# Attention loads of 256 tokens of one batch, and attention products on 64x64 tiles of TensorE

## The chip, the cores and the metric

The kernel runs on one core of a Trainium2 chip. The metric is the device time of one execution in microseconds, the median of several runs. The core has five engines that run their own instruction streams in order: TensorE (PE, the matmuls; its weight loads are listed apart as PEld), VectorE (DVE), ScalarE (ACT), GpSimd (POOL) and SyncE (SP, which here only issues DMAs). Matmuls write to PSUM, which has eight banks; the other data lie in SBUF, 128 partitions wide.

## The reference

A linear attention with decay (the RetNet recurrence) makes x, and a two-layer perceptron with a tanh gelu follows. There are 4 batches, 8 heads, 768 tokens and 64 elements a head, so 3072 rows of 512; the hidden width is 2048.

```python
for t in range(S):
    state = gamma * state + k[t] (outer) v[t]        # per batch and head, 64 x 64
    y[t] = scale * q[t] @ state
x = y as (batch * token, head * 64)
h = x @ w_in                                          # 512 -> 2048
g = 0.5 * h * (1 + tanh(c * (h + 0.044715 * h**3)))
out = g @ w_out                                       # 2048 -> 512
```

All inputs and the output are float32.

## The kernel before, in words

**Units of work.** The 768 tokens are cut into six chunks of 128. One chunk of all four batches (512 tokens) is one unit `c`. For each unit and batch, attention is done in chunked form: scores A = k q^T for all heads (`mm_A`, line 252), masked and scaled on VectorE into `a_sb` (`ev_A`, 265); the output Y is the sum of the carry product from the state `st` (`mm_yc`, 276) and the inner product of `a_sb` and v (`mm_yi`, 289), copied out to `xT` (`ev_Y`, 305 or 180/182); the new state is k^T v (`mm_s`, 313) added to the decayed old one (`ev_S`, 330). `att_AY` (348) issues the carry products of one pair of batches, the scores of another and the inner products in one go.

**Tiles on TensorE.** A head has 64 elements. The scores use two row halves of the array (64x128), inner products and states two column halves (128x64), the carry product the two diagonal 64x64 quarters. Each score matmul covers 128 keys and 128 queries of one head.

**Transposes.** Scores need q and k with the head's elements on the partitions. In units 0 and 1 TensorE transposes them (`mm_T`, 229). For q from unit 2 and for k from unit 3 on the load itself brings 32x32 blocks into place (`load_blk`, 106, 16 DMAs of 64 KB with runs of 128 bytes) and VectorE transposes within the blocks (238); k is then loaded a second time in its natural layout (`load1`, 100, runs of 256 bytes) for the states.

**The perceptron.** `moe1` (and `moe1_two`, on half the tokens) computes 128 columns of h in PSUM banks "h" (398) and ScalarE writes its gelu to `g` (414). Unit 0 multiplies by w_out directly (`moe2`, 432). From unit 1 on, `units_w` uses a Strassen-Winograd scheme: seven products of half size, each in two steps a = 0, 1 (536), over sums of g (`g_sums`, 476, on GpSimd, on VectorE in the last unit) and sums of w_out (`w_sums`, 469, VectorE). Step n = 2 is the first product that reads the sums.

**Order.** The order on each engine is written by hand. `run` (597) issues a list of TensorE units, and after unit i the entries of a table. The table of unit 1 (732 to 769) and the loop over units 2 to 5 (772 to 803) place the attention of the next unit and the preparation of the one after between matmuls of the perceptron. Scalings and casts of q, k and v (`prep1`, `prep_blk`) run on ACT, POOL and DVE. POOL's list at the end of unit 1 is: the sums, v of two batches, the last four sums, v of the other two, then v of unit 3.

**DMA queues.** Loads go through SP in order (some early ones through ACT), weights through POOL. At unit 0's end SP stores three output blocks (`ev_O`, 448 to 456) and goes on to load unit 2 at line 733. A one-element copy (`hold`, 130) makes the load of unit 1 wait until the third part of w_out has landed.

Of the kernel before, what the change touches and what calls it, by code (L numbers as in the profile page):

```python
# [16 lines left out]
def kernel(  # L17
# [12 lines left out]
    NCk = S // C  # L30
# [4 lines left out]
    assert Dh == 64 and d_model == H * Dh and B == 4 and NHP == 4 and NF == 16  # L35

    gam = 1.0 - 2.0 ** (-5.0 - np.arange(H, dtype=np.float64))
    p_i = np.arange(128, dtype=np.float64)  # L40
    qdec = gam[None, :] ** (p_i[:, None] - 32.0) * 0.125
    kdec = gam[None, :] ** (160.0 - p_i[:, None])
    g128 = gam ** 128.0
    gst = np.where(p_i[:, None] < 64, g128[None, 0::2], g128[None, 1::2])
    tri = (p_i[:, None] <= p_i[None, :]).astype(np.float64)

    j_p = np.arange(128)[:, None] // 64
    cst_np = np.concatenate([qdec, kdec, gst, tri], axis=1).astype(np.float32)
# [3 lines left out]
    hp_a, t_a = np.arange(NHP)[None, :, None], np.arange(128)[None, None, :]  # L52
    dec_np = 0.125 * gam[2 * hp_a + j_p[:, :, None]] ** (t_a - 32.0)
# [4 lines left out]
    ld = ctx.enter_context(tc.tile_pool(name="ld", bufs=2 * B))  # L58
    pre = ctx.enter_context(tc.tile_pool(name="pre", bufs=2 * B))
    att = ctx.enter_context(tc.tile_pool(name="att", bufs=4))  # L60
    xp = ctx.enter_context(tc.tile_pool(name="xp", bufs=1))
# [4 lines left out]
    OQ, OK, OG, OT = 0, H, 2 * H, 2 * H + NHP  # L66


    misc = const.tile([128, 32], F32)
    cst = const.tile([128, 192], F32)  # L70
    iden = const.tile([128, 128], F16)
    dec = const.tile([128, NHP, 128], F32)

    raw = {}
    srcs = {"q": q, "k": k, "v": v}

    BLK = {"q": (2, 3, 4, 5), "k": (3, 4, 5)}

    def ld_all(key):
        if key not in raw:
            raw[key] = ld.tile(
                [128, B * NHP, 4, 32],
                F32,
                tag=key[0],
                bufs=2 if key[0] == "q32" else 1,
                name=key[0],
            )
        return raw[key]  # L90

    def ld_tile(nm, c, b):
        if nm == "q":
            t = ld_all(("q32", c)).rearrange("p (b hp) a d -> p b (hp a d)", b=B)
            return t[:, b].rearrange("p (h d) -> p h d", h=H)
        if (nm, c, b) not in raw:
            raw[nm, c, b] = ld.tile([128, H, Dh], F32, tag=f"{nm}32", bufs=8, name=f"{nm}32")
        return raw[nm, c, b]

    def load1(eng, nm, c, b):  # L100
        eng.dma_start(  # L101
            out=ld_tile(nm, c, b),
            in_=srcs[nm][b, :, c * C:(c + 1) * C, :].rearrange("h p d -> p h d"),
        )

    def load_blk(nm, c):
        t = ld_all((nm + ("32" if nm == "q" else "T32"), c))
        src = srcs[nm].rearrange("b (hp j) s (dd d) -> j dd s (b hp) d", j=2, dd=2)
        for j in range(2):
            for dd in range(2):  # L110
                for a in range(4):
                    p0, t0 = (2 * j + dd) * 32, c * C + a * 32
                    nc.sync.dma_start(  # L113
                        out=t[p0:p0 + 32, :, a, :], in_=src[j, dd, t0:t0 + 32]
                    )

    def load(c):
        load_blk("q", c)
        if c in BLK["k"]:
            for b in range(B):  # L120
                load1(nc.sync, "v", c, b)
            load_blk("k", c)
            for b in range(B):
                load1(nc.sync, "k", c, b)
        else:
            for b in range(B):
                for nm in "kv":
                    load1(nc.sync, nm, c, b)

    def hold(nm, c, b, until):  # L130

        nc.gpsimd.tensor_copy(out=ld_tile(nm, c, b)[0:1, 0, 0:1], in_=until)

    nc.sync.dma_start(out=cst[:, :OT + 128], in_=cst_h.ap())
    load1(nc.scalar, "q", 0, 0)
    load1(nc.sync, "k", 0, 0)
    load1(nc.scalar, "v", 0, 0)
    nc.sync.dma_start(out=iden, in_=iden_h.ap())
    load1(nc.sync, "q", 0, 1)
    load1(nc.scalar, "k", 0, 1)  # L140
    load1(nc.sync, "v", 0, 1)
    load1(nc.sync, "k", 0, 2)
    load1(nc.sync, "q", 0, 3)
    load1(nc.sync, "v", 0, 3)


    zero = const.tile([128, 512], F16, name="zero")
    nc.vector.memset(zero, 0.0)  # L148
    nc.scalar.activation(
        out=misc[:, 0:1], in_=zero[:, 0:1], func=AF.Gelu_apprx_tanh, scale=1.0  # L150
    )

    def spin(n):
        ps = bank("h", shape=(128, 512), name="spin_ps")
        for _ in range(n):
            nc.tensor.matmul(  # L156
                out=ps, lhsT=zero[:, 0:128], rhs=zero, start=True, stop=True
            )


    st = const.tile([128, B, NHP, 64], F16, name="st")


    mask = const.tile([128, 2, NHP, 128], F32, name="mask")
    for j in range(2):
        for hp in range(NHP):
            nc.vector.tensor_scalar(
                out=mask[:, j, hp],
                in0=cst[:, OT:OT + 128],
                scalar1=float(1.0 / g128[2 * hp + j]),  # L170
                scalar2=None,
                op0=ALU.mult,
            )

    h16 = {}
    blk16 = {}

    def copy_on(eng, out, in_):
        if eng is nc.scalar:
            eng.copy(out=out, in_=in_)  # L180
        else:
            eng.tensor_copy(out=out, in_=in_)

    def prep1(eng, nm, c, b):
        t = pre.tile(
            [128, H, Dh], F16, tag=f"{nm}16", bufs=6 if nm == "q" else 2 * B, name=f"{nm}16"
        )
        src = ld_tile(nm, c, b)
        if (nm == "v") == (c < 2):
            copy_on(eng, t, src)  # L190
        else:
            col = OQ if nm == "q" else OK
            eng.tensor_tensor(  # L193
                out=t,
                in0=src,
                in1=cst[:, col:col + H].unsqueeze(2).broadcast_to([128, H, Dh]),
                op=ALU.mult,
            )
        h16[nm, c, b] = t

    def prep_blk(eng, nm, c, b):
        key, tag = ("q32", "q16") if nm == "q" else ("kT32", "kT16")
        t = pre.tile([128, NHP * 4, 32], F16, tag=tag, bufs=6 if nm == "q" else B, name=tag)
        copy_on(
            eng, t, ld_all((key, c))[:, b * NHP:(b + 1) * NHP].rearrange("p hp a d -> p (hp a) d")
        )
        blk16[nm, c, b] = t

    def pair(t, hp):
        return t[:, 2 * hp:2 * hp + 2]  # L210
# [6 lines left out]
    BANKS = {"h": 2, "o": 2, "att": 4}  # L217

    def bank(tag, dt=F32, shape=(128, NHP, 128), name="ps"):
        return psum.tile(list(shape), dt, tag=tag, bufs=BANKS[tag], name=name)  # L220

    def mm_T(c, b):
        parts = [(i, nm) for i, nm in enumerate("qk") if c not in BLK[nm]]
        if not parts:
            return
        ps = bank("att", F16, (128, 2, NHP, 128), "qkT_ps")
        for i, nm in parts:
            for hp in range(NHP):
                nc.tensor.transpose(  # L229
                    out=ps[:, i, hp], in_=pair(h16[nm, c, b], hp), identity=iden  # L230
                )
        pss["T", c, b] = ps

    def ev_T(c, b, eng=nc.vector):
        t = att.tile([128, 2, NHP, 128], F16, tag="qkT", name="qkT")
        for i, nm in enumerate("qk"):
            if c in BLK[nm]:
                nc.vector.transpose(  # L238
                    out=t[:, i].rearrange("p hp t -> p (hp t)"),
                    in_=blk16.pop((nm, c, b)).rearrange("p ha d -> p (ha d)"),  # L240
                )
        if ("T", c, b) in pss:
            i0 = sum(c in BLK[nm] for nm in "qk")
            copy_on(eng, t[:, i0:], pss.pop(("T", c, b))[:, i0:])
        qkT[c, b] = t

    def mm_A(c, b):
        t = qkT[c, b]
        ps = [bank("att", name=f"a_ps{j}") for j in range(2)]
        for hp in range(NHP):  # L250
            for j in range(2):
                nc.tensor.matmul(  # L252
                    out=ps[j][:, hp],
                    lhsT=t[j * 64:(j + 1) * 64, 1, hp],
                    rhs=t[j * 64:(j + 1) * 64, 0, hp],
                    start=True,
                    stop=True,
                )
        pss["A", c, b] = ps

    def ev_A(c, b):
        ps = pss.pop(("A", c, b))
        for j in range(2):
            s = att.tile([128, NHP, 128], F16, tag=f"a{j}", name=f"a_sb{j}")
            nc.vector.tensor_tensor(out=s, in0=ps[j], in1=mask[:, j], op=ALU.mult)  # L265
            a_sb[c, b, j] = s
# [567 lines left out]
```

## Time and profile before

| | us |
|---|---|
| median of 3 runs | 211.73 (211.6 to 213.02) |
| span of the profiled execution | 209.7 |
| TensorE busy | 200.6 |
| first projection matmul (unit 0) | 16.72 |
| output product of unit 0 begins | 32.92 |
| first projection of unit 1 | 51.94 |
| loops of units 2, 3, 4 and 5 begin | 88.15, 119.08, 149.66, 179.53 |
| last matmul ends | about 205.7 |
| one 128x512 sum on GpSimd / scaling of v | 1.15 / 1.04 |
| stream transposes on VectorE (28) | 19.1 in all |

The span is the time from the first to the last instruction of one profiled execution; the measured time is a little longer. In the timelines the first column is the start and the second the length of a merged piece; pieces of matmuls overlap a little, as their ends are modelled, so starts are compared with starts. "idle before" names how long the engine stood still and what released it.

| group | count | busy us | mean ns |
|---|---|---|---|
| projection (398) | 488 | 87.4 | 334 |
| scores (252), 64x128 tiles | 192 | 8.1 | 218 |
| carry (276), 64x64 tiles | 160 | 6.7 | 220 |
| inner (289), 128x64 tiles | 192 | 8.6 | 223 |
| states (313), 128x64 tiles | 160 | 5.1 | 198 |
| transposes (229) | 80 | 7.8 | 219 |

The mean of one matmul holds its way through the array; several are under way at once.

### The profile page before, as it was taken

The page shows a single profiled execution, that of the slowest core. Times are in us where ns is not written, and L with a number is a line of the kernel's source. Part 1 is how long each engine was busy: PE and PEld are TensorE (multiplying, and loading weights), DVE is VectorE, ACT ScalarE, POOL GpSimd, SP SyncE. Part 2 cuts the span into 40 slices and gives each one's busy share as a digit, 9 for nine tenths or more (in the row PEclk, how much of TensorE's full clock was granted, in tenths as well). Part 3 has the DMA queues.
Part 4 walks back from the last instruction along what each step waited for, and adds up shares of the span by engine and source line. Part 5 has one row for each costly group of instructions (what it writes and reads, how often), then busy time and mean ns, then how long its engine had stood idle before and what let it go on. Part 6 is the DMA issues. An engine that isn't in the chain of part 4 may idle for free.

```text
span 209.7 us, 4776 instructions
## 1 busy us (share of the span) xinstructions
PE 200.6 (96%) x1928; PEld 132.0 (63%) x1928; DVE 104.1 (50%) x213; ACT 101.9 (49%) x182; POOL 115.4 (55%) x120
## 2 busy tenths in 40 slices
PE   7789999999998999999999999999999999999992
PEld 3347644456786878844688744678644788545881
DVE  4445153478734649703857630867432784053430
ACT  2474563144458615168745266643365811566311
POOL 0596001133099999249998299997499980200000
PEclk9999999999999999999999999999999999999999
DMA  7999999998899798799798698796970000500004
GB/s 168 287 253 207 206 205 222 273 269 215 157 220 233 110 179 163 110 313 177 124 219 128 124 340 131 125 207 99 206 251 0 0 3 0 203 0 0 0 28 177
DMA packets 124438, 33.19 MB, mean 158 GB/s; under 512 B 117952, under 2 KB 122432, under 8 KB 124416
## 3 DMA queue, kind: packets, MB, share of 16 engines
q1 hardware_dynamic: 108272, 21.09, 50.3%
q0 software_dynamic: 5456, 8.65, 17.4%
q10 hardware_dynamic: 10688, 3.15, 6.4%
q8 instruction: 15, 0.25, 0.4%
q14 instruction: 7, 0.06, 0.1%
HBM read 30.78 MB, written 6.29 MB: 177 GB/s over the span
## 4 chain that ended last, share of the span: by engine, by line
PE 81%; SPq 6%; ACT 4%; DMA 4%; DVE 2%; issue 1%; ACTq 1%; DVEq 0%
PE h_ps L398 35%; PE o_ps L536 29%; SPq L113 5%; PE o_ps L432 5%; PE a_ps L252 3%; PE y_ps L289 3%; PE y_ps L276 2%; DMA iden<-rr_ident 2%; DMA v<-in_v_dram 2%; PE qkT_ps L229 2%; PE spin_ps L156 1%; SPq L101 1%; PE s_ps L313 1%; ACT g L414 1%; ACTq L101 1%
## 5 line engine op out<-in xcount | busy, mean ns | idle before, releaser
L398 PE MATMUL h_ps<-xT,w_in 128*128 128x512 f16 (+2 forms) x488 | 87.4, 334 | 0.5 <-ACT g L414 0.5
L414 ACT ACTIVATE g<-h_ps 128x512 f16<-128x512 f32 (+1 forms) x98 | 57.5, 589 | 33.9 <-PE h_ps L398 33.5
L398 PEld LDWEIGHTS <-w_in 128*128 128x128 f16 x488 | 45.3, 97 | 37.4 <-issue 2.8
L467 POOL TENSOR_TENSOR s_g<-g 128x512 f16<-128x512 f16 x32 | 36.9, 1152 | 9.4 <-ACT g L414 9.4
L265 DVE TENSOR_TENSOR a_sb<-a_ps,mask 128x512 f16<-128x512 f32 x48 | 30.1, 682 | 23.1 <-PE a_ps L252 23.1
L536 PEld LDWEIGHTS <-s_g 128*128 128x128 f16 x320 | 30.2, 98 | 4.3
L536 PE MATMUL o_ps<-t_w,s_g 128*128 128x256 f16 x240 | 27.8, 273 | 0.0
L536 PEld LDWEIGHTS <-g 128*128 128x128 f16 x240 | 23.4, 98 | 3.6
L467 POOL TENSOR_TENSOR s_g<-s_g,g 128x512 f16<-128x512 f16 x16 | 18.4, 1153 | 1.3
L536 PE MATMUL o_ps<-w_out,g 128*128 128x256 f16 x160 | 18.6, 273 | 0.0
L467 POOL TENSOR_TENSOR s_g<-g,s_g 128x512 f16<-128x512 f16 x16 | 18.5, 1153 | 0.0
L193 POOL TENSOR_TENSOR k<-k,cst 128x512 f16<-128x512 f32 x8 | 8.3, 1044 | 17.3 <-DMA k<-in_k_dram 17.3
L569 POOL DMA_DIRECT2D out_dram<-o_sb x8 | 5.9, 737 | 20.3 <-DVE o_sb L467 16.8
L193 POOL TENSOR_TENSOR v<-v,cst 128x512 f16<-128x512 f32 x16 | 16.2, 1044 | 0.0
L238 DVE STREAM_TRANSPOSE qkT<-kT 128x512 f16<-128x512 f16 x12 | 8.1, 678 | 15.0 <-ACT kT L180 9.5
L565 ACT COPY o_sb<-o_ps 128x512 f32<-128x512 f32 (+1 forms) x5 | 2.7, 543 | 25.1 <-PE o_ps L536 25.1
L432 PE MATMUL o_ps<-w_out,g 128*128 128x512 f16 x64 | 14.8, 380 | 0.0
L305 DVE TENSOR_TENSOR xT<-y_ps,dec 128x512 f16<-128x512 f32 x16 | 10.3, 686 | 4.5 <-PE y_ps L289 4.5
L238 DVE STREAM_TRANSPOSE qkT<-q 128x512 f16<-128x512 f16 x16 | 11.0, 690 | 2.6 <-ACT q L180 2.5
L559 ACT COPY s_u<-o_ps 128x512 f32<-128x512 f32 (+1 forms) x6 | 3.1, 514 | 17.6 <-issue 9.9
L330 DVE SCALAR_TENSOR_TENSOR st<-st,cst,s_ps 128x128 f16<-128x128 f16 (+1 forms) x40 | 10.1, 313 | 2.0 <-PE s_ps L313 2.0
L156 PE MATMUL spin_ps<-zero 128*128 128x512 f16 x32 | 9.4, 429 | 1.2 <-DVE zero L148 1.2
(55 smaller groups left out, 185.3 us busy)
## 6 DMA issues: line engine op xcount, KB each, us to landing
k<-in_k_dram SPq DMA_DIRECT2D x22, 256.0 KB, 4.7
v<-in_v_dram SPq DMA_DIRECT2D x18, 256.0 KB, 4.0
q<-in_q_dram SPq DMA_DIRECT2D x64, 64.0 KB, 2.8
out_dram<-o_sb POOLq DMA_DIRECT2D x8, 512.0 KB, 5.2
kT<-in_k_dram SPq DMA_DIRECT2D x48, 64.0 KB, 2.7
w_in<-in_moe_w_in_dram POOLq DMA_DIRECT2D x4, 512.0 KB, 9.3
w_out<-in_moe_w_out_dram POOLq DMA_DIRECT2D x4, 512.0 KB, 14.7
v<-in_v_dram ACTq DMA_DIRECT2D x6, 256.0 KB, 5.5
```

The lines of the kernel that those rows point to most:

```text
L113: nc.sync.dma_start(out=t[p0:p0 + 32, :, a, :], in_=src[j, dd, t0:t0 + 32])
L156: nc.tensor.matmul(out=ps, lhsT=zero[:, 0:128], rhs=zero, start=True, stop=True)
L193: eng.tensor_tensor(out=t, in0=src, in1=cst[:, col:col + H].unsqueeze(2).broadcast_to([128, H, Dh]), op=ALU.mult,)
L238: nc.vector.transpose(out=t[:, i].rearrange("p hp t -> p (hp t)"), in_=blk16.pop((nm, c, b)).rearrange("p ha d -> p (ha d)"),)
L265: nc.vector.tensor_tensor(out=s, in0=ps[j], in1=mask[:, j], op=ALU.mult)
L305: nc.vector.tensor_tensor(out=x, in0=ps, in1=dec, op=ALU.mult)
L330: nc.vector.scalar_tensor_tensor(out=t[:, :, hp], in0=t[:, :, hp], scalar=cst[:, OG + hp:OG + hp + 1], in1=s_ps[:, :, hp], op0=ALU.mult, o ...
L398: nc.tensor.matmul(out=out, lhsT=w_in_sb[wi][:, kc, wr * 128:(wr + 1) * 128], rhs=xT[c][:, kc, t0:t1], start=(kc == 0), stop=(kc == NHP - ...
L414: nc.scalar.activation(out=out, in_=in_, func=AF.Gelu_apprx_tanh, scale=1.0)
L432: nc.tensor.matmul(out=ps[:, n0:n1], lhsT=g_sb[c, fc // 8][:, fc % 8, b * C:(b + 1) * C], rhs=w_out_sb[fc // (NF // NO)][:, fc % (NF // NO ...
L467: eng.tensor_tensor(out=out, in0=in0, in1=in1, op=op)
L536: nc.tensor.matmul(out=po, lhsT=lhs(c, lk, fp, a), rhs=rhs(rk, fp), start=(new and fp == 0 and (last or a == 0)), stop=(stop and fp == NP ...
```

## The change

**Units and loads.** A unit `m` is now 256 tokens of two batches (`pb`): units 0 and 1 cover the first 256 tokens, 2 and 3 the next, 4 and 5 the last. A load brings 256 tokens of one batch: partition p holds the neighbouring tokens 2p and 2p + 1 (r = 0, 1), so a run is 512 bytes and a load 512 KB. Partitions 0 to 63 are the first chunk of 128 tokens (cc = 0), 64 to 127 the second. `load_blk` and the second load of k are gone, and so are the VectorE transposes.

**Transposes.** In units 0 and 1 TensorE transposes q and k as before. From unit 2 on q and k are cast and SP issues a transposing DMA from SBUF to SBUF for each (16 of 256 KB).

```diff
+    def T_dma(nm, m, bi):
+        SY.dma_start_transpose(out=qk_tile(m, bi)[:, "qk".index(nm)], in_=h_tile(nm, m, bi))
```

**Products.** A chunk's keys (and queries) of one parity r and half cc are 64 long. Scores, inner products and states are matmuls with 64 rows and 64 columns, in the order x, r, j, cc, so that four in a row lie on four quarters of the array. There are twice as many as before; the carry product keeps its count.

```diff
+    QUADS = [(x, r, j, cc) for x in range(2) for r in range(2) for j in range(2) for cc in range(2)]
+
+    def A_mm(m, bi, us=(0, 1)):
+        t = qk_tile(m, bi)
+        for u in us:
+            ps = [bank("att", shape=(128, 2, 2, 128), name=f"a_ps{j}") for j in range(2)]
+            pss["A", m, bi, u] = ps
+            for x, r, j, cc in QUADS:
+                n = 2 * (2 * u + x)
                 nc.tensor.matmul(
-                    out=ps[j][:, hp],
-                    lhsT=t[j * 64:(j + 1) * 64, 1, hp],
-                    rhs=t[j * 64:(j + 1) * 64, 0, hp],
+                    out=ps[j][half(cc), x, r],
+                    lhsT=t[half(j), 1, n + r, half(cc)],
+                    rhs=t[half(j), 0, n:n + 2, half(cc)],
                     start=True,
                     stop=True,
                 )
```

Because carry and inner products write the same bank from different row halves, a one-element copy on ACT or DVE now reads the bank after the last carry product, and the first inner product waits for it:

```diff
+        dst, src = misc[0:1, 1:2], ys[1][0:1, NHP - 1, 0:1]
+        seen = eng.copy(out=dst, in_=src) if eng is AC else eng.tensor_copy(out=dst, in_=src)
+        needs(seen, ins)
+        behind[m, bi] = seen
```

`slot` takes the place of `att_AY`: carry of (m, bi), scores of another half, inner products, copies out, masks. The state step of both chunks is `S_mm` and `S_ev` (tensor_tensor operations where scalar_tensor_tensor stood); `v` is decay-scaled in place of k, the mask is one triangle for all heads, and `xT` has two buffers.

**Order.** The tables are rewritten. Unit 0's output product runs in the order of halves n = 0, 1, then 2, 3 (before: 0, 1, 2 side by side, then 3). Loads of (2, 0), (2, 1) and (3, 0) stand on SP behind unit 0's stores and ahead of the first transposes. Those of unit 1:

```diff
+    loads(2, 0)
+    loads(2, 1)
+    loads(3, 0)
     run(
...
         {
+            2: [(slot, 1, 1, "o", VE, None, None, (VE, AC))],
+            3: [(g_sums, PO, 1, 0, 4, 0, 1), (casts, VE, 2, 0), (T_dmas, 2, 0)],
+            6: [(casts, VE, 2, 1), (T_dmas, 2, 1), (loads, 3, 1)],
             7: [(g_sums, PO, 1, 4, 8, 0, 1)],
+            10: [(att_A, 2, 0)],
+            11: [(g_sums, PO, 1, 0, 4, 1, 2)],
+            12: [(scale_v, PO, 2, 0)],
+            15: [(g_sums, PO, 1, 4, 8, 1, 2), (scale_v, PO, 2, 1)],
         },
     )
     run(
         units_w(1),
         {
+            0: [(casts, AC, 3, 0), (T_dmas, 3, 0), (loads, 4, 0)],
+            2: [(casts, AC, 3, 1), (T_dmas, 3, 1), (loads, 4, 1)],
+            4: [(att_S, 2)],
+            6: [(slot, 2, 0, "h", AC, 2, 1), (scale_v, PO, 3, 0)],
+            9: [(slot, 2, 1, "h", AC, 3, 0), (scale_v, PO, 3, 1)],
+            13: [(att_S, 3)],
         },
     )
```

and those of the loop over units 2 to 5:

```diff
         for i in range(4):
+            more(4 * i + 3, (g_sums, PO if n < NM else VE, c, 2 * i, 2 * i + 2))
+        if n < NM:
+            more(6, (slot, n, 0, "o", VE, n, 1))
+            more(22, (slot, n, 1, "h", AC, m, 0))
+        if m < NM:
+            more(15, (casts, AC, m, 0), (T_dmas, m, 0))
+            more(23, (casts, AC, m, 1), (T_dmas, m, 1))
+            more(15, (scale_v, PO, m, 0), (scale_v, PO, m, 1))
+            more(28, (att_S, m))
+        if m + 1 < NM:
+            more(15, (loads, m + 1, 0))
+            more(23, (loads, m + 1, 1))
```

## The prediction

> **What bounds the kernel now.** I read the page's busy shares first, then the chain of waits, then TensorE's timeline, and last the timelines of the engines that feed it.
>
> ```profile
> PE 200.6 (96%) x1928; PEld 132.0 (63%) x1928; DVE 104.1 (50%) x213; ACT 101.9 (49%) x182; POOL 115.4 (55%) x120
> ...
> PE 81%; SPq 6%; ACT 4%; DMA 4%; DVE 2%; issue 1%; ACTq 1%; DVEq 0%
> ```
>
> TensorE is busy 96% of 209.7 us, so time is won only by shortening its stream and lost by any new wait in it. TensorE's timeline, start and length in us:
>
> ```profile
> 51.94 1.92 PE L398 MATMUL h_ps<-xT,w_in 128*128 128x256 f16 x16
> ...
> 76.47 0.63 PE L276 MATMUL y_ps<-qkT,st 64*64 64x128 f16 x16
> 77.03 0.62 PE L252 MATMUL a_ps<-qkT 64*128 64x128 f16 x16
> 77.58 0.64 PE L289 MATMUL y_ps<-a_sb,v 128*64 128x128 f16 x16
> 78.15 2.79 PE L536 MATMUL o_ps<-t_w,s_g 128*128 128x256 f16 x24
> 80.88 0.44 PE L313 MATMUL s_ps<-v,k 128*64 128x64 f16 x16
> 81.25 1.92 PE L536 MATMUL o_ps<-t_w,s_g 128*128 128x256 f16 x16
> ...
> 87.99 4.39 PE L398 MATMUL h_ps<-xT,w_in 128*128 128x512 f16 x19
> ```
>
> Read start to start. 16 attention matmuls take 0.55 us. Elsewhere 8 of the same take 0.33 us (chain of waits), so 8 more cost 0.22: two tiles run together, 55 ns a pair, plus about 0.11 us whenever the tile shape changes. The state products (64 columns) take 0.25 for 8 and 0.37 for 16: 31 ns a pair. A projection unit of 8 matmuls of 256 columns takes 0.875 us.
>
> Two feeders run with no slack beside this: GpSimd and the load queue.
>
> ```profile
> 57.45 1.14 POOL L467 TENSOR_TENSOR s_g<-g 128x512 f16<-128x512 f16 x1 [5.71 <-ACT g L414]
> ...
> 71.56 2.05 POOL L193 TENSOR_TENSOR v<-v,cst 128x512 f16<-128x512 f32 x2
> ...
> 77.02 1.15 POOL L467 TENSOR_TENSOR s_g<-g,s_g 128x512 f16<-128x512 f16 x1
> 78.13 6.05 POOL L193 TENSOR_TENSOR v<-v,cst 128x512 f16<-128x512 f32 x6
> ```
>
> From 57.45 GpSimd is packed: 16 sums at 1.13 us, with two v scalings before the last four sums. Its sums end at 78.13, and TensorE reads them at 78.15. The state products at 80.88 read the v scaled at 71.56. SyncE's queue:
>
> ```profile
> 44.10 1.77 SPq L455 DMA_DIRECT2D out_dram<-o_sb  x3
> 45.92 0.82 SPq L732 DMA_DIRECT2D dec<-rr_dec  x1
> 46.83 10.59 SPq L113 DMA_DIRECT2D q<-in_q_dram  x16
> 57.47 0.49 SPq L101 DMA_DIRECT2D k<-in_k_dram  x1
> ```
>
> Loads for chunk 2 start behind the third store, at 46.83, 22.5 us before TensorE's first score product of that chunk (69.33).
>
> **Work on TensorE.** Scores, inner outputs and states go from pairs to twice as many matmuls on four tiles; the carry product stays in pairs. If four run as one, the four-tile group streams in 55 ns what the pair did; if only pairs overlap it takes 110. The tightest spacing in the trace is 15 to 16 ns a matmul (states), four of which make 62 ns: I take 60. The TensorE work of the second stage (start of unit 1's first projection, 51.94, to the loop, 88.15: 36.2 us) becomes: 30 projection units at about 0.87 = 26.2; the second half's outputs of unit 1, 0.9; scores of (2,0), 0.6; two slots of carry 0.44 + scores 0.48 + inner 0.48 + switches 0.15 = 3.1; two state products of 64 matmuls, 16 x 31 to 62 ns, 0.9 each with switches. Sum 32.6, so 3.6 less than now. The saving is k's transposes (0.23 each, with waits of 0.45, 0.32 and 0.48 before them) and tile-shape switches that vanish because carry, scores and inner outputs now share one shape.
>
> A rule speaks against the change here. The Trainium skill (TensorE: Matmul & The Clock Gate, Part 3) lets a weight load overlap a running matmul only where the row group differs, and two of the four tiles share a row group. In this trace the inner outputs and states share all rows, differ in column half only, and still run as pairs at 55 and 31 ns: measurement and rule differ, the measurement decides for two tiles, and nothing here shows four.
>
> **New wait 1: transposes behind loads.** From unit 2 on, q and k are transposed by DMA on SyncE's queue. For (2,0) they stand behind nine loads of 512 KB, which stand behind the third store of unit 0. That store now follows the 15th of 16 output steps, so the loads start only 1.7 us before unit 1's first projection (call its start T): after that step come the copy 0.6 and store issue 0.6 on one side, and slot 1.45 + last step 0.86 + states 0.6 on TensorE. Scores of (2,0) are wanted after 11 projection steps and the slot: T + 10.5. The queue is first in, first out by the chain's own row for the 32 KB identity matrix, which took 4.28 us behind larger loads. Rate: loads of 256-byte runs reach 287 GB/s (5 to 10 us). Queue 10 (nearly all 256-byte) spends 20 ns a packet; taking these out of queue 1 leaves about 12.4 for 128 bytes; the line gives 33.7 ns at 512, so 1.16 times the rate: 330 GB/s. Nine loads take 14.3 us. No row shows a DMA transpose: bounds are the plain rate (0.8 us each) and the slow 128-byte loads (16 x 64 KB in 10.59 us, so 2.65 us each). I take the plain one. Landing: T - 1.7 + 2 (start and landing) + 14.3 + 1.6 = T + 16.2: TensorE waits 5.7 us. For the transpose's price the Trainium skill has two answers: "TRN2 transpose DMAs are as fast as regular DMAs" (Advanced Engine Details and Errata, X-Bar Transpose), which gives the sum above, and 1309 ns per 128x128 block (VectorE: DVE Perf Modes, The three transpose paths), which for eight blocks in turn would be an estimated 10.5 us each, 168 us for the sixteen, and a kernel far above 250 us; no run here shows either.
>
> **New wait 2: states behind GpSimd.** The states of unit 2 now stand after the fifth output step of unit 1 and read v of (2,1), whose scaling is GpSimd's last piece after all 16 sums. Were TensorE never to wait, it would come there at T + 20.4 (16 projection steps 14.0, slot 0.9, scores 0.6, five output steps 4.35, the first batch's states 0.55). GpSimd starts at T + 5.3 (four steps 3.5, slot 0.9, gelu and hand-over 0.9), does 16 x 1.13 + 2 x 2.05 = 22.2 plus 0.4 of waiting as now: T + 27.9, 7.5 us late even without wait 1. With wait 1 the third group of sums starts after its gelu at T + 16.2 + 0.6 + 0.875 + 0.65 = T + 18.3, and GpSimd ends 13.2 us later (9.1 of sums, 4.1 of v): T + 31.5. Both waits together cost 31.5 - 20.4 = 11.1.
>
> After idling TensorE is slow: the spin matmuls at the start come every 0.43 us for 2.5 us, then every 0.22. Two such restarts: the first delays GpSimd about 0.7, the second costs 1.3.
>
> **The three loops.** The third output product reads GpSimd's sums pair by pair. TensorE reaches its seventh pair at 18.9 + 0.65 us from a loop's start (16 projections 13.8, one slot 1.55, four output steps 3.5, six matmuls 0.65), but GpSimd, with an unchanged start of 4.3 and 14 sums, is ready at 20.4 (now 108.53 - 88.15). What scores and slots save ahead of that point is lost to it; behind it stands as much as now. Loops: 30.7, 30.6, 29.5 against 30.93, 30.58, 29.87, so -0.5.
>
> **Start.** First projection now at 16.72. Bytes ahead of the first 256 tokens are the same 1.5 MB and the k cast of (0,1) stands on ScalarE ahead of the first outputs' copies; longer runs save about a microsecond of loading, bigger pieces lose it again. The weights still pace the reload of unit 1 (GpSimd's wait for w_out, 14.44 us). VectorE must wait for bigger q tiles before the transposes of (1,1). T = 52.5, between 50 and 55: +0.6.
>
> The added one-element reads between carry and inner products are hidden under scores or a projection step in nine slots and bare in three, about 0.2 us each (the 128x1 ACTIVATE takes 0.20): +0.6. They queue on ScalarE and VectorE in order, behind a cast at most. Removed and hidden: VectorE's stream transposes (28, 19 us), the second load of k, the smaller packets; none is on the path now.
>
> Sum: 0.6 - 3.6 + 11.1 + 2.0 - 0.5 + 0.6 = +10.2. Span 209.7 becomes 219.9; the median stands 2.0 above the span: 221.9, rounded to 221.5.
>
> **Rivals.**
> 1. Transposes in time, GpSimd alone late: loads above 450 GB/s or overtaken in the queue. 7.5 + 1.3 in place of 13.1: 217. Against: the identity row. 0.12.
> 2. Slow transposes (2.65 us): wait 1 grows by 3.7, and in two loops scores of the next unit wait 1.6 each: 228. 0.12, of which 0.02 for transposes slower still, by which the loops themselves would wait. The skill's 1309 ns belongs to that last case.
> 3. Four tiles go as two pairs, 110 ns: 192 groups of scores and inner outputs + 50 ns = 9.6, states little; a third is hidden before GpSimd's two points: 228 to 231. The skill's row-group rule above would do this or worse. 0.10.
> 4. Faster: neither wait comes, TensorE keeps its 3.6 and the loops' 0.5. This decides if GpSimd ends by T + 20.4, i.e. sums and scalings at two thirds of their present time, or TensorE comes 7 us later for a cause that does not prolong the rest, and the transposes land by T + 10.5: 211.7 + 0.6 - 3.6 - 0.5 + 0.6, about 209. For it: lighter DMA and VectorE. Against: GpSimd's rows are its own speed, not waiting. 0.10.
> 5. Part of this, within 1% of 211.7: 0.06.
>
> The forecast keeps 0.50. Slower by over 1% (about what a measurement can tell from no change): 0.50 + 0.12 + 0.12 + 0.10 = 0.84; faster 0.10; same 0.06. Range 214 to 231: it holds cases 1 to 3 and the start's spread, and leaves out 4 and 5.
>
> **What would show it.** TensorE idle before the first four-tile scores of unit 2 until a DMA, about 6 us; idle in the states of unit 2 until GpSimd, about 5 us; four-tile score groups of 32 in about 0.5 us; in the loops short waits for GpSimd's sums. A stage from T to the loop of 45 us is right, 33 wrong. If TensorE comes to the states after GpSimd, or transposes land within 4 us of their cast, the forecast falls.

## The result, and the profile after

The changed kernel takes 236.88 us (median of 4 runs, 235.65 to 237.8) against 212.38 us of the kernel before beside it (4 runs, 211.6 to 213.15): a ratio of 1.116, 95% interval 1.110 to 1.122. It is slower, as forecast, but by 24.5 us and not by 10; the time lies above the range of 214 to 231. Experiment 11 alone had slower executions (three of ten, at 217 us and more); its time below is the median of the other seven.

The profiled execution spans 233.9 us (before: 209.7). The page's busy times and its chain of waits:

```profile
PE 203.4 (87%) x2440; PEld 134.2 (57%) x2440; DVE 93.4 (40%) x173; ACT 95.1 (41%) x158; POOL 110.0 (47%) x101
...
PE 51%; POOL 22%; DMA 17%; DVE 3%; SPq 2%; ACT 2%; issue 1%; POOLq 0%; DVEq 0%
```

TensorE does about as much work as before (203.4 us against 200.6) but holds only 51% of the chain, where it held 81%; GpSimd and DMA take 39% of it. Where the time went, by starts of TensorE's pieces in the two timelines:

| from, to | before us | after us | difference |
|---|---|---|---|
| start to unit 0's output product | 32.92 | 34.57 | +1.65 |
| to unit 1's first projection (T) | 19.02 | 25.10 | +6.08 |
| T to the loop of unit 2 | 36.05 | 50.65 | +14.60 |
| loops of units 2, 3, 4 | 30.92, 30.59, 29.86 | 31.44, 31.46, 30.63 | +2.16 |
| the last unit, to the end of the span | 30.34 | 30.05 | -0.29 |

The loop starts given at the top for the kernel before, and taken over by the prediction (36.2 us for T to the loop), are those of the chain of waits, 0.16 to 0.17 us later than in the timeline; the table reads both kernels in the timeline.

TensorE's timeline of the changed kernel (start, length, engine and line, operation, and in brackets the idle time before it and what ended it):

```profile
59.67 2.83 PE L401 MATMUL h_ps<-xT,w_in 128*128 128x256 f16 x24
...
79.24 1.07 PE L227 MATMUL a_ps<-qkT 64*64 64x128 f16 x32 [7.59 <-DMA qkT<-q]
80.24 5.39 PE L401 MATMUL h_ps<-xT,w_in 128*128 128x256 f16 x40
...
95.77 0.64 PE L270 MATMUL s_ps<-v,k 64*64 64x64 f16 x32 [5.40 <-POOL v L137]
96.35 3.24 PE L540 MATMUL o_ps<-t_w,s_g 128*128 128x256 f16 x16
...
110.32 6.26 PE L401 MATMUL h_ps<-xT,w_in 128*128 128x512 f16 x28
...
131.28 2.14 PE L540 MATMUL o_ps<-t_w,s_g 128*128 128x256 f16 x18 [1.18 <-POOL s_g L137]
```

T is 59.67. The two forecast waits stand in the second stage, at 79.24 for the DMA that transposes q, and at 95.77 for GpSimd's v. After each, TensorE runs slow: the 32 scores at 79.24 take 1.00 us up to the next piece (0.57 in experiment 1 below), and the 16 matmuls of 256 columns at 96.35 take 3.17 instead of 1.75. The mean granted clock of this stage, as a share of TensorE's full speed, is 0.87, where it was 1.00 before. In each of the three loops a wait of 1.16 to 1.18 us for GpSimd's sums is new.

SyncE's queue (the first two columns are start and length of the issue, stalls included):

```profile
46.34 10.49 SPq L463 DMA_DIRECT2D out_dram<-o_sb  x3
56.88 0.43 SPq L93 DMA_DIRECT2D k<-in_k_dram  x1
...
70.05 1.51 SPq L93 DMA_DIRECT2D v<-in_v_dram  x1
71.66 4.10 SPq L216 DMA_TRANSPOSE qkT<-k  x1
75.86 1.36 SPq L216 DMA_TRANSPOSE qkT<-q  x1
```

The loads start at 56.88 behind the third store, 2.8 us before T. The ninth is issued at 70.05, and only then the two transposes, as the program orders them.

GpSimd's timeline:

```profile
75.12 1.15 POOL L137 TENSOR_TENSOR s_g<-g,s_g 128x512 f16<-128x512 f16 x1
82.84 1.15 POOL L137 TENSOR_TENSOR s_g<-g 128x512 f16<-128x512 f16 x1 [6.58 <-ACT g L417]
...
92.71 1.15 POOL L137 TENSOR_TENSOR s_g<-g,s_g 128x512 f16<-128x512 f16 x1
93.82 6.07 POOL L137 TENSOR_TENSOR v<-v,cst 128x1024 f16<-128x1024 f32 x3
```

GpSimd itself stands still for 6.58 us, because TensorE, waiting for the transposes, produces no h from which ScalarE could make g. It then works without a gap to the v that TensorE waits for at 95.77. So GpSimd can't use the first wait to catch up, and the second comes nearly whole on top of it: 5.40 us here, 5.96 in experiment 1, where most of the first is gone.

### The profile page after: what moved, and what is told of

Same layout as the page of the kernel before. It is cut to its first block, busy times and chain, and to the rows that moved or that the text cites. A ratio compares the mean times of both kernels' runs of the same rounds, so it can differ in the third digit from the quotient of the medians.

```text
span 233.9 us, 5567 instructions
## 1 busy us (share of the span) xinstructions
PE 203.4 (87%) x2440; PEld 134.2 (57%) x2440; DVE 93.4 (40%) x173; ACT 95.1 (41%) x158; POOL 110.0 (47%) x101
## 3 DMA queue, kind: packets, MB, share of 16 engines
q0 software_dynamic: 5456, 8.65, 16.2%
## 4 chain that ended last, share of the span: by engine, by line
PE 51%; POOL 22%; DMA 17%; DVE 3%; SPq 2%; ACT 2%; issue 1%; POOLq 0%; DVEq 0%
PE h_ps L401 20%; PE o_ps L540 20%; POOL s_g L137 18%; DMA w_out<-in_moe_w_out_dram 6%; DMA v<-in_v_dram 5%; PE a_ps L227 3%; POOL v L137 2%; DMA k<-in_k_dram 2%; PE o_ps L435 2%; PE y_ps L332 2%; PE y_ps L313 2%; SPq L216 2%; DMA q<-in_q_dram 2%; DVE a_sb L137 2%; PE s_ps L270 1%
## 5 line engine op out<-in xcount | busy, mean ns | idle before, releaser
L401 PE MATMUL h_ps<-xT,w_in 128*128 128x512 f16 (+1 forms) x480 | 87.2, 339 | 2.5 <-DMA w_in<-in_moe_w_in_dram 0.9
L417 ACT ACTIVATE g<-h_ps 128x512 f16<-128x512 f32 x96 | 57.4, 598 | 46.7 <-PE h_ps L401 46.7
L137 DVE TENSOR_TENSOR a_sb<-a_ps,cst 128x512 f16<-128x512 f32 x48 | 29.8, 680 | 12.8 <-PE a_ps L227 12.7
L540 PE MATMUL o_ps<-t_w,s_g 128*128 128x256 f16 x240 | 29.7, 281 | 3.5 <-POOL s_g L137 3.5
L137 POOL TENSOR_TENSOR v<-v,cst 128x1024 f16<-128x1024 f32 (+1 forms) x14 | 23.4, 1685 | 18.3 <-DMA v<-in_v_dram 18.3
L540 PE MATMUL o_ps<-w_out,g 128*128 128x256 f16 x160 | 18.3, 273 | 0.0
L132 ACT CAST k<-k 128x1024 f16<-128x1024 f32 (+1 forms) x11 | 10.1, 928 | 17.1 <-DMA k<-in_k_dram 17.1
L227 PE MATMUL a_ps<-qkT 64*64 64x128 f16 x384 | 10.2, 234 | 7.8 <-DMA qkT<-q 7.6
L137 DVE TENSOR_TENSOR o_sb<-o_ps,s_p 128x512 f32<-128x512 f32 (+1 forms) x6 | 3.6, 602 | 30.9 <-ACT s_p L563 22.3
L227 PEld LDWEIGHTS <-qkT 64*64 64x64 f16 x384 | 7.8, 115 | 10.3 <-DMA qkT<-k 7.0
L270 PE MATMUL s_ps<-v,k 64*64 64x64 f16 x320 | 5.5, 199 | 7.1 <-POOL v L137 6.1
```

What stands on the lines that cost most here:

```text
L137: eng.tensor_tensor(out=out, in0=in0, in1=in1, op=op)
L227: nc.tensor.matmul(out=ps[j][half(cc), x, r], lhsT=t[half(j), 1, n + r, half(cc)], rhs=t[half(j), 0, n:n + 2, half(cc)], start=True, stop= ...
L270: nc.tensor.matmul(out=ps[cc][half(j), i, hp], lhsT=kk[half(cc), hp, r, j], rhs=vv[half(cc), hp, j, r], start=(r == 0), stop=(r == 1), ski ...
L401: nc.tensor.matmul(out=out, lhsT=w_in_sb[wi][:, kc, wr * 128:(wr + 1) * 128], rhs=xT[c][:, kc, t0:t1], start=(kc == 0), stop=(kc == NHP - ...
L417: nc.scalar.activation(out=out, in_=in_, func=AF.Gelu_apprx_tanh, scale=1.0)
L540: nc.tensor.matmul(out=po, lhsT=lhs(c, lk, fp, a), rhs=rhs(rk, fp), start=(new and fp == 0 and (last or a == 0)), stop=(stop and fp == NP ...
```

## The experiments

All start from the changed kernel; T and the loop's start are read from TensorE's timeline. Ratios are against the kernel before.

**1. Transposes ahead of the later loads.**

```diff
     loads(2, 0)
-    loads(2, 1)
-    loads(3, 0)
+    for nm in "kq":
+        load(SY, nm, 2, 1)
...
-            3: [(g_sums, PO, 1, 0, 4, 0, 1), (casts, VE, 2, 0), (T_dmas, 2, 0)],
-            6: [(casts, VE, 2, 1), (T_dmas, 2, 1), (loads, 3, 1)],
+            3: [(g_sums, PO, 1, 0, 4, 0, 1), (casts, VE, 2, 0), (T_dmas, 2, 0), (load, SY, "v", 2, 1)],
+            6: [(casts, VE, 2, 1), (T_dmas, 2, 1), (loads, 3, 0), (loads, 3, 1)],
```

The casts and transposes of unit 3 move from output steps 0 and 2 to 2 and 5.

> The loads of v of (2,1) and of (3,0) move on SyncE's queue behind the first transposes, so that these stand behind five loads in place of nine; the casts of unit 3 move two and three output steps later, nothing is left out. Theory (the transposes were late because of what stood ahead of them, and the sums on GpSimd were late because TensorE's projections were): TensorE's wait before the scores of (2,0) falls from 7.6 us to under 2, GpSimd's third group of sums starts that much earlier, the wait in the states of unit 2 stays at 6 to 8 us, and the time falls by about 7 us, to 230. Rival 1 (the transposes themselves are slow): the wait stays above 5 us, the time within 2 us of 236.9. Rival 2 (GpSimd alone sets the end of this stage, whatever TensorE does before): the wait in the states grows to about 13 us and the time stays at 236 to 237.

228.8 us; ratio 1.077 (1.071 to 1.083). TensorE's timeline:

```profile
73.30 0.64 PE L227 MATMUL a_ps<-qkT 64*64 64x128 f16 x32 [1.40 <-DMA qkT<-q]
...
89.41 0.64 PE L270 MATMUL s_ps<-v,k 64*64 64x64 f16 x32 [5.96 <-POOL v L137]
...
103.96 2.37 PE L401 MATMUL h_ps<-xT,w_in 128*128 128x512 f16 x10
```

The first wait falls from 7.59 to 1.40 us and the loop starts 6.4 us sooner at the same T. Place in the queue made that wait. The second stays: the v that TensorE waits for now comes at T + 29.5, where it came at T + 36.1.

**2. v of unit 2 on VectorE.** Both `scale_v(PO, 2, ...)` entries become `VE`.

> The scaling of v of (2,0) and (2,1) goes from GpSimd to VectorE, at the same places of the program. Theory (the states of unit 2 wait for GpSimd's list, of which these scalings are 3.8 us and the last piece): the wait of 5.4 us in the states is gone, the wait of 7.6 us before the scores stays, and the time falls by about 6 us, to 231. Rival (the sums themselves are late, and TensorE waits for them one step later instead): the next step waits 3 us or more for the fourth group of sums, and the time falls by under 3 us.

229.33 us; ratio 1.080 (1.074 to 1.086). The wait before the states is gone and no other for GpSimd stands in its place in this stage; the one for the transposes is 7.13 us, and the loop starts at 104.14 (T is 60.01). GpSimd's last piece of work was the whole second wait.

**3. Both.**

> Both of the edits before. Theory (two waits in one chain, both on the path): the stage from unit 1's first projection to the loop, 50.65 us, becomes 34 to 36, with at most 2 us of waiting for the fourth group of sums; the time is 221 to 223, which is what the start and the three loops lose against the kernel before the change. Rival (a third cause is hidden behind the two): the stage stays above 39 us.

224.29 us; ratio 1.056 (1.049 to 1.062). The gains of 1 and 2, 8.1 and 7.6 us, come to 12.6 together. In the traces they nearly add: T to the loop falls from 50.65 us to 44.04, 44.13 and, with both, 38.50, so by 6.6, 6.5 and 12.15. 1.0 us is missing, less than two smaller waits that come up next:

```profile
85.98 1.48 PE L540 MATMUL o_ps<-t_w,s_g 128*128 128x256 f16 x12 [1.40 <-POOL s_g L137]
...
89.57 0.64 PE L332 MATMUL y_ps<-a_sb,v 64*64 64x128 f16 x32 [1.09 <-ACT misc L322]
...
99.04 6.26 PE L401 MATMUL h_ps<-xT,w_in 128*128 128x512 f16 x28
```

Even without v, GpSimd's 16 sums are now read as they end, and the one-element read stands behind a cast on ScalarE. T to the loop is 2.45 us longer than before; the 34 to 36 us expected were missed, and the rival's 39 was not reached.

**4. Weights ahead on GpSimd's queue.** In the start stage `scale_v(PO, 0, 1, ...)` becomes `VE`, so that GpSimd issues the weights without waiting for v of (0,1).

> The scaling of v of (0,1) goes from GpSimd to VectorE, so that GpSimd's six remaining weight loads no longer stand behind the 512 KB load of this v, which landed at 16.8 us. Theory (the first projection of unit 1 came 7.7 us later than before the change because the loads of unit 1 wait for the third part of w_out, which was issued late): w_out's third part lands near 33 us in place of 36.1, the loads of unit 1 start 3 us earlier, and so do the projections of unit 1 and the end: 234. Rival (the loads of unit 1 are simply too large for the place where they are wanted, or the weights take the bandwidth of v): unit 1 starts within 1 us of 59.7 and the time stays.

232.7 us; ratio 1.098 (1.090 to 1.106). GpSimd's `hold` read, which releases the reload of unit 1, in this kernel's timeline:

```profile
32.70 0.44 POOL L101 CAST q<-w_out 1x1 f32<-1x1 f16 x1 [14.90 <-DMA w_out<-in_moe_w_out_dram]
```

It was at 36.17 in the changed kernel and 33.36 before. T falls from 59.67 to 56.79.

**5. The loops alone.**

```diff
-        tt(eng, t[3], q[0, 0], q[0, 1], ALU.subtract)
+        tt(VE if c > 1 else eng, t[3], q[0, 0], q[0, 1], ALU.subtract)
...
-            more(6, (slot, n, 0, "o", VE, n, 1))
+            more(7, (slot, n, 0, "o", VE, n, 1))
```

> One thing is changed, in the three loops over units 2 to 4 (and partly 5): the first slot stands after projection unit 7 instead of 6, so that the gelu of unit 7 no longer waits for the slot, and the third of the four sums of g goes from GpSimd to VectorE for units from 2 on. Theory: the 1.16 to 1.18 us of TensorE idling before the third output product in each loop come from GpSimd's second group of sums starting late and from its 14 to 16 sums of 1.14 us; with both eased the three waits vanish, the loops take about 30.2, 30.2 and 29.5 us instead of 31.4, 31.5 and 30.6, and the time is 233 to 234 us. Rival: the sums are not what bounds the loops; VectorE's 16 more operations beside GpSimd's slow both (the 0.69 us cast took 1.63 beside a GpSimd sum) and the slot's copies come late, so another wait of about 1 us stands in each loop, and the time is 236 to 238 us.

232.27 us; ratio 1.093 (1.088 to 1.099). Loops of 30.54, 30.58 and 29.74 us instead of 31.44, 31.46 and 30.63; the third product runs through:

```profile
128.38 2.78 PE L540 MATMUL o_ps<-t_w,s_g 128*128 128x256 f16 x24
```

The waits are gone, for 0.9 us each (the run doesn't say which of its two edits did it); a shorter one, for a read behind a sum on VectorE, took part of the gain. T was 58.50 in this profile without any edit ahead of it, so 1.2 us of the difference between the spans is spread of the start (58.5 to 60.5 over the kernels that leave the start alone).

**6. The reload of unit 1**, on top of 4: `hold` waits for the second part of w_out instead of the third, and `prep_0(1, 1)` stands ahead of the state step of (1,0).

> On top of the kernel with the scaling of v(0,1) on VectorE (232.7 us, unit 1's first projection at 56.79): the reload of unit 1 waits for the second part of w_out instead of the third, and q of (1,1) is scaled before the state step of (1,0) instead of behind it. Theory: the first stage is late because unit 1's 512 KB pieces land late and because the q scaling stands behind the state step (TensorE idles 1.27 us for it); the loads start about 1.5 us sooner, unit 1's first projection comes at 54 to 55.5 us, and the time is 230 to 231.5 us. Rival: the load is bound by the DMA rate that it shares with the rest of w_out; what starts sooner lands no sooner, the last weights land later, and the first projection of unit 1 stays at 56 to 57.5 us, the time at 232 to 234 us.

231.05 us; ratio 1.087 (1.081 to 1.092). T is 55.27. The q scaling now meets GpSimd's v (see the last section), and TensorE still waits 0.57 us for it.

**7. All of these together.**

> All the single edits together: transposes of unit 2 ahead of the later loads, scaling of v of unit 2 and of (0,1) on VectorE, the two edits of the loops, the two edits of unit 1's reload. If each gain is that of a wait of its own, the sum is 236.9 - 12.6 (both waits of the second stage) - 4.2 (weights) - 3.4 (loops) - 1.5 (reload) = 215 us, between 213 and 218: about 1.5% slower than the kernel before, whose start and loops are then the whole of the rest. Rival: the gains share a wait (VectorE's added work meets GpSimd's, or a reload that comes sooner only waits at the next place), and the time stays at 219 to 222 us.

217.75 us; ratio 1.024 (1.018 to 1.030): inside what was expected if the gains add, though 2.6 us above their sum of about 215. T is 55.20, the loop starts at 96.0. The waits left in between were 2.46 us (transposes, behind two more loads), 0.54 (sums) and 2.04 (the read behind a cast that waited for its load).

**8. Another order inside the groups.**

```diff
-    QUADS = [(x, r, j, cc) for x in range(2) for r in range(2) for j in range(2) for cc in range(2)]
+    QUADS = [(x, r, j, cc) for cc in range(2) for x in range(2) for r in range(2) for j in range(2)]
```

> Only the order of the matmuls within the scores and the inner outputs is changed, so that cc, the half of the chunk pair, is the outermost index. Neighbours in the scores then lie on different row halves and the same column half, and neighbours in the inner outputs on the same row half and different column halves; four in a row no longer cover the four quarters. Theory (TensorE works in the given order, and what overlaps are neighbours on different quarters): groups of 32 take about 0.88 us instead of 0.45 (55 ns a pair), for scores and inner outputs alike, and the time rises by 3 to 8 us to 240 to 245 us. Rival a (TensorE's queue looks far enough ahead, or one column half after the other is no limit): both stay at 0.45 us and the time at 236 to 238 us. Rival b (only tiles of different row halves overlap, the rule on row groups): the scores take 0.88 us, but the inner outputs run one at a time, about 1.76 us for 32, and the time is above 247 us.

236.83 us; ratio 1.114 (1.110 to 1.118), the time of the changed kernel. The first slot of a loop on TensorE:

```profile
117.89 0.67 PE L227 MATMUL a_ps<-qkT 64*64 64x128 f16 x30
118.36 0.67 PE L332 MATMUL y_ps<-a_sb,v 64*64 64x128 f16 x32
118.97 7.99 PE L401 MATMUL h_ps<-xT,w_in 128*128 128x512 f16 x36
```

From its carry products (117.44) to the next projection the slot takes 1.53 us; in the changed kernel 1.46 (116.51 to 117.97). Rival a holds. In this order eight score matmuls stand in a row on one column half (eight inner products on one row half) before the next eight take the other, and that costs 0.07 us a slot.

**9. A better order of the second stage**, on top of 7: loads of (2,1) and (3,0) behind the transposes of (2,0), casts and transposes of (2,1) five steps later, loads of (3,1) behind them; casts of (2,0) ahead of the sums, casts of (3,1) behind the first slot; `t[3]` on VectorE for unit 1 too; the slot's read on ScalarE in the loops.

> On top of all single edits together (217.8 us): loads of (2,1) and (3,0) are issued behind the transposes of (2,0) and those of (3,1) behind the transposes of (2,1); the casts of (3,1) on ScalarE stand behind the first slot of unit 2 instead of ahead of it; the third sum of g goes to VectorE for unit 1 too; the reads of the first slot in the loops go from VectorE to ScalarE. Theory: the waits left in that kernel's second stage were 2.46 us for the transposes of (2,0), 0.54 for GpSimd's sums and 2.04 for ScalarE's read behind a cast that waited for its load, with about 1.6 us of slower TensorE after them, and each loop loses about 0.35 us for a read that stands behind a sum on VectorE; without them the time is 217.8 - 6.6 - 1.0 = 210 us, between 209 and 213, about that of the kernel before. Rival: what is taken off GpSimd and ahead of the queue comes back on VectorE (sums, casts, v and masks in one queue, slowed beside GpSimd) or as late loads of (3,1); a wait of 2 to 4 us takes their place and the time is 213 to 217 us.

216.03 us; ratio 1.016 (1.013 to 1.020): the rival. TensorE's timeline:

```profile
79.55 0.65 PE L270 MATMUL s_ps<-v,k 64*64 64x64 f16 x32 [2.57 <-DVE v L137]
...
89.23 0.64 PE L227 MATMUL a_ps<-qkT 64*64 64x128 f16 x32 [1.27 <-DMA qkT<-q]
...
94.49 7.12 PE L401 MATMUL h_ps<-xT,w_in 128*128 128x512 f16 x32
```

The wait for the transposes of (2,0) is gone, but VectorE, which got v, is 2.57 us late with it, and the transposes of (3,0), now behind the loads of (3,1), 1.27. T is 55.22, T to the loop 39.3, the loops 30.2, 30.2 and 29.3.

**10. Transposes on TensorE**, one part undone: from unit 2 on `att_T` in place of `T_dmas`, one step ahead of the scores that read it.

> One part of the change undone, all else as in the changed kernel (236.9 us): from unit 2 on q and k are transposed by TensorE and copied out by VectorE, as in units 0 and 1, instead of by DMA. Theory (TensorE waited 7.59 us for the scores of (2,0) because their transposes stood behind nine loads; the loads of (2,0) themselves land in time): that wait falls below 1 us; TensorE gets 8 groups of 16 transposes of about 0.95 us, of which some 2 us hide under the loops' waits for GpSimd; GpSimd's wait before the states of unit 2 stays at 4 to 6 us; together -7.6 + 5.5, 233 to 236 us. Rival a: it was the loads of (2,0) that were late, and the wait for them stays above 4 us: 239 to 243 us. Rival b: VectorE, with 16 more copies of 0.64 us beside its masks, sets the end of the loops: more than 240 us, with waits for VectorE before scores or states in every loop.

236.74 us; ratio 1.116 (1.109 to 1.122): the time of the changed kernel, just above what was expected. The first wait is gone (0.18 us for VectorE's copy is left); the loads themselves were in time. The second remains:

```profile
89.04 0.65 PE L270 MATMUL s_ps<-v,k 64*64 64x64 f16 x32 [5.96 <-POOL v L137]
...
105.86 4.53 PE L401 MATMUL h_ps<-xT,w_in 128*128 128x512 f16 x20
```

The loop starts 4.5 us sooner, and the loops, of 33.2, 33.2 and 31.5 us, give it back. So the DMA transposes are worth 1.8, 1.8 and 0.9 us in the three loops, and cost as much as all of that once, where they stand behind the loads.

**11. A last step**, on top of 9: v of (1,1) and of (2,1) earlier on VectorE, casts of (2,1) on ScalarE, loads of (3,1) behind the transposes of (3,0) and their casts behind the second slot.

> On top of the kernel with 216.0 us: VectorE is relieved where it met GpSimd or was late. The scaling of v(1,1) goes from GpSimd to VectorE behind the copies of the transposes of (1,1), so that the q scaling of (1,1) no longer runs beside GpSimd (3.06 us there against 1.42 alone); the casts of (2,1) go to ScalarE; v(2,1) is scaled ahead of the last sum on VectorE; the loads of (3,1) are issued behind the transposes of (3,0), their casts behind the second slot. Theory: the first projection of unit 1 comes about 1.5 us sooner (53.5 to 54), and of the waits left in the second stage, 2.57 us for v on VectorE and 1.27 for the transposes of (3,0), some 3 us go; the time is 211 to 213 us, that of the kernel before. Rival: the casts on ScalarE delay the gelus and so TensorE as much as they relieve VectorE, or the loads of (3,1) are now late for the loop; 214 to 217 us.

214.64 us; ratio 1.010 (1.007 to 1.014): the rival's size. Its profiled execution was its longest (218.94 us), so it can say which waits there are and not what they cost in the others: 1.28 us for a state step on VectorE, 0.99 for GpSimd's v, and in the loop 2.10 for the transposes of (3,1). Each piece that is moved off one late queue is late on the next. No version here is faster than the kernel before.

## Why the prediction was wrong in size

Three steps of the sum failed: the start, by 7.1 us, the size of the two waits in the second stage, by 4.35 with what hangs on them, and the loops, by 2.65 and in sign. The waits themselves came where they were forecast.

**Start (T = 52.5; measured 59.67, +7.1 beyond the forecast).** This step failed most: "The weights still pace the reload of unit 1" was right, "bigger pieces lose it again" was not worked out. GpSimd issues the weights, and two of four parts of w_in and all of w_out now stand behind its scaling of v(0,1), whose load lands at 16.79. The prediction followed SyncE's queue and not GpSimd's. GpSimd's timeline, two lines of the kernel before and two of the changed one:

```profile
15.88 3.04 POOL L388 DMA_DIRECT2D w_out<-in_moe_w_out_dram  x4
...
33.36 0.44 POOL L132 CAST q<-w_out 1x1 f32<-1x1 f16 x1 [14.44 <-DMA w_out<-in_moe_w_out_dram]
```

```profile
16.87 2.04 POOL L137 TENSOR_TENSOR v<-v,cst 128x512 f16<-128x512 f32 x2 [3.65 <-DMA v<-in_v_dram]
...
36.17 0.44 POOL L101 CAST q<-w_out 1x1 f32<-1x1 f16 x1 [12.80 <-DMA w_out<-in_moe_w_out_dram]
```

The issues of w_out, from 15.88 to 18.92 us before, are now from 20.39 to 23.37; its third part is in 2.8 us later, and the reload of unit 1 with it. Experiment 4 gives 2.9 us back; its T of 56.79 lies 1.7 us below the lowest of the seven kernels that leave the start alone (58.50 to 60.54). The rest stands in waits of TensorE; that the size of the pieces is their cause was not tested. TensorE waits 1.73 us for k of (1,0), 0.82 for q of (1,1), 0.87 for w_in and 0.86 for an output copy in unit 0, and 0.94 for masks before the states. Experiment 6 won 1.5 of this (T is 55.20 to 55.27 in the three kernels 6, 7 and 9 that share its start). 3.3 us were not removed by any run, and their cause stays open.

**TensorE's stream of the second stage (32.6; held).** Its busy time is 36.3 of 50.65 us. The slow stretches behind the two waits explain about 2.9 of it (0.43 in the scores, 0.85 in the projection after them, 1.6 in the states and the 16 matmuls after them), which leaves 33.4; 32.6 and 0.6 of reads were in the sum. Four-tile groups go at 55 ns (32 scores in 0.45 us) and about 34 ns (64 states in 0.65 us, less the 0.11 for a change of tile shape) where 60 was taken. Rival 3, two pairs, falls.

On this the Trainium skill has two rules. TensorE: Matmul & The Clock Gate, Part 3, lets a weight load overlap a matmul only in another row group, in its list of what overlaps; TensorEngine Tiling (Array Packing), Key Properties, says that different tiles load and multiply in parallel. The changed kernel's 55 ns a group of four, and experiment 8, where the order made no difference, agree with the second and not with the first.

**Wait 1 (5.7; measured 7.59).** Right in kind, too small in its parts. The transposes landed at T + 19.6, not T + 16.2. Nine loads at 294 GB/s (slices of the profile's page) instead of 330 take 16.0 us, not 14.3; two transposes, issued 1.4 us apart and each some 3.3 from issue to landing, take 4.4 (what is left) instead of 1.6; the loads started 1.1 us sooner than taken. That is +1.7 + 2.8 - 1.1 = +3.4. TensorE came later as well, since its own small waits (0.64 for an output copy, 0.24 for the read) were not in the sum.

The transpose's price lies between the two that the prediction named from the Trainium skill. Advanced Engine Details and Errata (X-Bar Transpose) says as fast as regular DMAs, which at 294 GB/s would be 0.9 us for 256 KB; VectorE: DVE Perf Modes (The three transpose paths) has 1309 ns a block, an estimated 10.5 us for eight. The trace has 1.4 us from issue to issue. Rival 2, 2.65 us each with loops that wait for them, falls: no loop of the changed kernel waits for a transpose. Rival 1's own condition was set too low: at 450 GB/s the nine loads take 10.5 us, and by the prediction's sum the transposes land at T + 12.4, still 1.9 late.

**Wait 2 (both together 11.1; measured 13.0).** The chain was right: third group of sums after the late gelu, then 13.2 us of GpSimd (measured 12.9, from 82.84 to 95.77). It began at T + 23.2 instead of T + 18.3: 3.4 of that is wait 1's miss, 0.4 the slow scores, 0.85 the first projection unit, whose gelu starts 1.93 us after the unit does (1.09 in experiment 1). Experiments 1 and 2 show the two causes, 3 that they nearly add. Rival 1 would have had the first wait vanish: it took an edit to bring it to 1.40. The restarts cost 2.9 us, not 2.0, and their price is not steady: the slow stretch behind the first wait is 1.3 us here, and 2.8 in experiment 5 behind a wait of nearly the same length (7.94).

**Loops (-0.5; measured +2.16).** This step failed in its sign. "GpSimd, with an unchanged start of 4.3 and 14 sums, is ready at 20.4": the second group of sums needs the gelu of unit 7, which now stands behind the slot at 6, so GpSimd pauses (0.41 us), and the seventh pair is ready at 20.96 and not 20.4 from the loop's start (131.28), while TensorE, with its saving, is there 1.18 sooner. Experiment 5 moves the slot and takes a quarter of the sums away: 0.9 us a loop. With experiment 9 the loops are 30.2, 30.2 and 29.3, 0.4 to 0.75 us shorter than before. The attention groups take 3.65 us in the second of them instead of 3.99, so the four-tile products do save, once nothing eats it; in the first, another 0.34 us of the difference lies in 52 projection matmuls that took 11.79 us before, and 11.45 in the next loop.

**Sum.** T 7.1, second stage 50.65 against 46.3 with the reads (4.35), loops 2.65, the last unit -0.1 (30.05 against the 30.17 by the prediction's starts): 14.0 us, the difference of the spans (233.9 and 219.9). The median stands 3.0 above the span, 2.0 were taken; the profiled execution was the fastest of the four. The forecast's 221.5 is 0.4 below its own sum of 221.9.

Rivals 4 and 5 fall: both waits came, and removing them (3) doesn't reach the time of before. The sign had two sufficient causes among those forecast, either of them worth more than the 3.6 us that TensorE was to save. It had a third that the forecast left out: with both waits eased (3) the span is still 12.9 us above that of before, and 8.6 of these are the start (T 60.54 against 51.94).

## What to carry to other kernels

When pieces get bigger, follow every queue on which a piece now stands ahead of something else, also the issues of DMAs behind a computation: here a v scaling ahead of the weights cost 2.9 us, and nine loads ahead of two transposes 6 to 8. When a wait also stops the engine that is waited for next, that engine can't catch up, so the two waits nearly add: follow them along the chain. And a new wait's price is its landing time under the load that surrounds it, not the transfer's own time.

## What the hardware showed unexpectedly

**VectorE and GpSimd stop each other.** The timelines of the changed kernel, VectorE and then GpSimd:

```profile
50.54 0.42 DVE L137 TENSOR_TENSOR stt<-s_ps,stB 128x256 f32<-128x256 f32 x1
50.99 1.22 DVE L137 TENSOR_TENSOR stA<-stt,cst 128x256 f16<-128x256 f32 x1
```

```profile
50.03 1.90 POOL L137 TENSOR_TENSOR v<-v,cst 128x1024 f16<-128x1024 f32 x1 [3.48 <-DMA v<-in_v_dram]
```

A state step from SBUF to SBUF takes 1.22 us instead of 0.42 and ends, at 52.21, 0.28 after GpSimd's v (51.93); the step before it, which reads PSUM, takes 0.42 in the same shadow. In experiment 6 the four q scalings, 1.42 us alone (52.14 in the changed kernel), meet v at 46.15 to 48.19:

```profile
46.02 3.12 DVE L137 TENSOR_TENSOR q<-q,cst 128x256 f16<-128x256 f32 x4
```

GpSimd loses as well: its sums take 1.59 to 1.60 us instead of 1.15 beside VectorE's casts. The Trainium skill (SBUF — State Buffer, SBUF: two separate sides) describes a port pair of the two engines that one holds for a whole instruction while the other blocks; the end times here fit that, to some tenths of a us. Work moved to VectorE meets this too: in experiment 9 the casts of (2,1), ahead of the v that TensorE waits for, take 1.18 and 1.64 us beside GpSimd's sums, where the changed kernel's take 0.69 with GpSimd idle.

**TensorE's tiles take their matmuls ahead of the order.** In experiment 8 eight matmuls on one half of the array stood ahead of eight on the other, and a slot took 1.53 us instead of 1.46; in pairs its 64 score and inner matmuls alone would take an estimated 1.76 us (32 pairs of 55 ns). In the changed kernel's slot four scores start at 116.82 and 116.90 us, while the last four carry products, which stand ahead of all scores in the program, start at 116.87 and 116.92. How far ahead this goes was not tried.
